# Long-context attention and a phase-mixing block: batch 0's q and k and the token weights turned by quarters of the array, and the opening put in another order

## The chip, the cores and the metric

The kernel runs on one core of one Trainium2 chip. Five engines work side by side, each through its own instructions in their written order: TensorE (PE, matmuls and transposes, with its weight loads shown apart as PEld), VectorE (DVE), ScalarE (ACT), GpSimd (POOL) and SyncE (SP). DMAs are issued from the queues of SP, ACT and POOL. The metric is device time in microseconds, lower is better. Three runs of the kernel before took 171.09, 171.58 and 172.12 us, so the median is 171.58.

## The reference

Inputs are q, k, v of shape [4 batches, 8 heads, 768 positions, 64], the weights w_theta and w_ch [512, 512] and the token weights w_tok_r and w_tok_i [768, 768]. The output is float32 [4, 768, 512].

```
scores = q @ k^T / 8 - slope[h] * dist        # keep: the first 8 keys, and the 96 keys up to the query
a      = softmax(where(keep, scores, -1e9));  x = a @ v, heads side by side: [4, 768, 512]
theta  = x @ w_theta;  zr = x*cos(theta);  zi = x*sin(theta)
y      = w_tok_r @ zr + w_tok_i @ zi          # over positions
u      = x + y;  out = u + relu(u @ w_ch)
```

## The kernel before

Positions are tiled by 128 (NT = 6 tiles), heads by pairs, so a pair of heads fills 128 partitions. Each batch goes through attention, theta, the token mix and the channel mix. Batches 1 to 3 run their attention beside the token mix of the batch before (`attend_beside`); batch 0's attention, its theta stage and the setup of the token weights stand alone at the beginning, in an order written out by hand (lines 533 to 603). All calls go through `K = tc.keep_in_program_order`, so each engine executes in the order of the source.

For each pair of heads, `att_transpose` (line 209) turns q and k with PE transposes into PSUM tiles `ps_tr` (two buffers) and copies them to the SBUF tile `qk`, reordering positions. For batch 0 (lines 238 to 250) one PSUM tile holds q and one holds k; each is filled by 12 transposes of 128x64, ACT copies k and DVE copies q. For later batches (lines 216 to 237) the array is used in quarters: 48 transposes of 64x64, one PSUM tile for each half of the partitions, each tile holding half of q and half of k. `att_extras` (line 254) then copies the middle key tiles with the 8 global keys put in front (`mT`), on POOL as a rule.

`att_scores` (line 279) works in three groups of score blocks. Group 0 needs `kT` and `qT` alone, groups 1 and 2 need `mT` as well. In batch 0, groups 0 and 2 get the distance bias by a matmul (`att_bias`, line 266, with `ident_d` as weights) and ACT's exp gives the probabilities; group 1 gets exp on ACT and then a product with `wmask` on DVE (`att_mul`, line 311). Scores lie in the wide PSUM tiles `ps_w` (two buffers). `prepare_v` (line 88) copies v for the same global keys. `att_values` (line 325) multiplies probabilities and v into `ps_mm` (two buffers), `att_norm` (line 358) divides on DVE, `turn_x` (line 368) transposes x for `mix_theta` (line 387). `mix_z` (line 407) forms z on DVE from ACT's sines.

`setup_wtok` (line 108) turns one 128-row strip `st` of a token matrix by six 128x128 transposes and copies it by one copy, on DVE for the first matrix and parts of the second, on ACT for strips 0 and 1 of the second. `mix_tok` (line 421) consumes the strips. In the order written out, the transposes of one lot lie between matmuls that need an earlier lot.

Loads go mostly by POOL's queue, which also computes; the first pair's q and k come by SP's and ACT's queues (line 141). `keep_warm` issues matmuls on zeros.

Of the kernel before, what the change touches and what calls it, by code (L numbers as in the profile page):

```python
# [10 lines left out]
BF = mybir.dt.bfloat16  # L11
# [5 lines left out]
def kernel(  # L17
# [13 lines left out]
    nc = tc.nc  # L31
    B, H, S, D = q.shape
    T = 128
# [74 lines left out]
    def setup_wtok(wi, st, eng, spare):  # L108
        if not spare:
            pt = ps_tr(S)  # L110
        else:
            pt = psum.tile([T, S], BF, name="ps_mm", tag="ps_mm", bufs=2)
        for tt in range(NT):
            K(nc.tensor.transpose(pt[:, tt * T:(tt + 1) * T],  # L114
                                  w_nats[wi][:, tt, st * T:(st + 1) * T], ident))
        if eng == "dve":
            K(nc.vector.tensor_copy(out=w_tokT[wi][:, st, :], in_=pt))  # L117
        else:
            K(nc.scalar.copy(out=w_tokT[wi][:, st, :], in_=pt))
# [21 lines left out]
    for src, dst, queue in ((q, first[:, 0], nc.sync), (k, first[:, 1], nc.scalar)):  # L141
        K(queue.dma_start(out=dst, in_=src[0, 0:2].rearrange("h (p t) d -> p h (t d)", t=NT)))
# [7 lines left out]
    keep_warm(8)  # L150
# [58 lines left out]
    def att_transpose(b, h0, extras=True, sins=None, q_eng="dve", between=None, cuts=(T,)):  # L209

        qk = abuf.tile([T, 2 * S + (NT - 2) * T], BF, name="qk", bufs=2)
        kT, qT = qk[:, 0:S], qk[:, S:2 * S]
        qTs[b, h0], kTs[b, h0] = qT, kT
        mTs[b, h0] = qk[:, 2 * S:]
        copy = nc.scalar.copy if q_eng == "act" else nc.vector.tensor_copy
        if b > 0:

            HP = T // 2
            halves = [ps_tr(S), ps_tr(S)]
            for t_ in range(NT):  # L220
                for i_, src in enumerate((k_sb[b], q_sb[b])):
                    c = (i_ * NT + t_) * HP
                    for r in range(2):
                        P = slice(r * HP, (r + 1) * HP)
                        for hh in range(2):
                            K(nc.tensor.transpose(  # L226
                                halves[r][hh * D:(hh + 1) * D, c:c + HP],
                                src[P, h0 + hh, t_ * D:(t_ + 1) * D], ident[P, P]))
            if sins is not None:
                sins()  # L230
            for r, op in enumerate((nc.scalar.copy, copy)):
                K(op(out=qk[:, 0:2 * S].rearrange("a (i r p t) -> a i r p t",  # L232
                                                  i=2, r=2, t=NT)[:, :, r, :, :],
                     in_=halves[r].rearrange("a (i t p) -> a i p t", i=2, t=NT)))
            if extras:
                att_extras(b, h0)
            return
        pq, pk = ps_tr(S), ps_tr(S)
        for src, pst in ((q_sb[b], pq), (k_sb[b], pk)):
            if pst is pk and between is not None:  # L240
                between()
            for t_ in range(NT):
                for hh in range(2):
                    K(nc.tensor.transpose(pst[hh * D:(hh + 1) * D, t_ * T:(t_ + 1) * T],
                                          src[:, h0 + hh, t_ * D:(t_ + 1) * D], ident))

        for op, dst, src in ((nc.scalar.copy, kT, pk), (copy, qT, pq)):
            for p0, p1 in zip((0,) + cuts, cuts):
                K(op(out=dst.rearrange("a (p t) -> a p t", t=NT)[:, p0:p1, :],  # L249
                     in_=src.rearrange("a (t p) -> a p t", t=NT)[:, p0:p1, :]))  # L250
        if extras:
            att_extras(b, h0)

    def att_extras(b, h0, eng=nc.gpsimd, values=True):
        kT = kTs[b, h0]
        mT = mTs[b, h0]
        K(eng.tensor_copy(out=mT, in_=kT[:, T:S - T]))  # L257
        K(eng.tensor_copy(
            out=mT.rearrange("a (t p) -> a t p", p=T)[:, :, 0:NG],
            in_=kT[:, None, 0:NG].to_broadcast([T, NT - 2, NG])))  # L260
        if eng is nc.gpsimd and values:
            prepare_v(b, h0)
# [16 lines left out]
    def att_scores(b, h0, g_, mul=True):  # L279
# [3 lines left out]
        bias = b == 0 and g_ != 1  # L283
# [249 lines left out]
    for h in range(H):  # L533
        make_wmask(h)
# [3 lines left out]
    att_transpose(0, 0, extras=False, between=lambda: keep_warm(1), cuts=(43, T))  # L538
    make_ident_d(2, 6)
    att_extras(0, 0, nc.vector)  # L540
    prepare_v(0, 0, nc.vector)
    keep_warm(1)
    att_scores(0, 0, 0)
    att_scores(0, 0, 1)
    att_transpose(0, 2, extras=False)
# [4 lines left out]
    for h0 in (2, 4, 6):  # L550
        att_scores(0, h0, 0)
        att_scores(0, h0, 1, mul=False)
        att_values(0, h0 - 2, apart=True)
        att_norm(0, h0 - 2)
        att_norm(0, h0 - 1)
        if h0 < 6:
            att_transpose(0, h0 + 2)
            if h0 == 2:
                load_wtok(1)
            else:  # L560
                load_heads(1, 0, 4)
        att_mul(0, h0, 1)
        att_scores(0, h0, 2)
        if h0 < 6:
            turn_x(0, h0 // 2 - 1, False)
# [101 lines left out]
```

## Time and profile before

| what | value |
|---|---|
| median of three runs | 171.58 us (171.09 to 172.12) |
| the profiled execution's own time | 171.33 us |
| its span, first to last instruction | 169.5 us |
| granted TensorE clock | 1.0 |
| busy: PE, DVE, ACT, POOL | 158.7, 114.7, 103.0, 63.2 us |
| DMA moved | 24.08 MB, mean 142 GB/s |
| first scores of batch 1 begin | 39.47 us |

The profile is of one execution. A line of the timeline gives start, duration, engine, source line, operation, output tile and input tiles, how many instructions were merged, and in brackets the idle time before the first of them with what ended it. The chain of waits follows the end of the program back to its start: each piece is work, or the idle time that the next piece had to wait for ("issue"). A time to landing is counted from a DMA's issue. Busy shares are averages over stages with different limits.

### The profile page before, as it was taken

To read this page: it belongs to the slowest core of one execution; us is meant where nothing else is said; L and a number is where in the kernel's file an instruction comes from. 1 tells how busy PE (TensorE), PEld (TensorE's weight loads), DVE (VectorE), ACT (ScalarE), POOL (GpSimd) and SP (SyncE) were. 2 spreads that over 40 slices of the span, in tenths; PEclk is the share of its full clock that TensorE was granted. 3 is DMA by queue.
4 is the path that set the end of the run, shared out by engine and by line. 5 is a ranking of instruction groups with operands and counts; after the bars stand their busy time and mean duration, and the time that the engine had idled before them with its cause. 6 is when DMAs were issued, how large, how long until landed. Compare 5 with 4: busy or idle time off the path is not lost.

```text
span 169.5 us, 4624 instructions
## 1 busy us (share of the span) xinstructions
PE 158.7 (94%) x1965; PEld 86.2 (51%) x1988; DVE 114.7 (68%) x210; ACT 103.0 (61%) x120; POOL 63.2 (37%) x99
## 2 busy tenths in 40 slices
PE   7779999999899999999999999999999999999992
PEld 2346665555465654446555554445655544444440
DVE  7768875965858875767587694849568756534362
ACT  4989887957686562798658615996765618300010
POOL 8996797004484650032972900054245000000000
PEclk9999999999999999999999999999999999999999
DMA  4999999999999999910599999711953342121325
GB/s 148 194 180 190 209 211 208 198 180 182 158 140 196 141 173 215 257 70 4 92 145 170 155 187 197 210 62 37 73 110 95 99 148 86 68 60 34 113 102 186
DMA packets 57060, 24.08 MB, mean 142 GB/s; under 512 B 43088, under 2 KB 54096, under 8 KB 57040
## 3 DMA queue, kind: packets, MB, share of 16 engines
q0 software_dynamic: 35328, 12.45, 65.5%
q1 hardware_dynamic: 21440, 10.95, 31.2%
q10 hardware_dynamic: 272, 0.39, 0.7%
q8 instruction: 15, 0.25, 0.6%
q14 instruction: 5, 0.04, 0.1%
HBM read 25.69 MB, written 6.29 MB: 189 GB/s over the span
## 4 chain that ended last, share of the span: by engine, by line
PE 80%; DVE 6%; DMA 4%; issue 3%; POOL 3%; ACT 3%; DVEq 0%; ACTq 0%; POOLq 0%
PE ps_mm L430 35%; PE ps_mm L472 12%; PE ps_w L395 11%; PE ps_w L297 7%; PE ps_w L346 5%; DMA v_sb<-in_v_dram 4%; PE ps_tr L226 3%; PE ps_mm L346 2%; ACT e L306 2%; PE ps_tr L114 2%; DVE zri L411 1%; DVE w_tokT L117 1%; PE ps_tr L378 1%; DVE p L319 1%; ACT qk L249 1%
## 5 line engine op out<-in xcount | busy, mean ns | idle before, releaser
L430 PE MATMUL ps_mm<-zri,w_tokT 128*128 128x512 bf16 x276 | 67.0, 380 | 1.3 <-issue 0.8
L306 ACT ACTIVATE e<-ps_w 128x1024 bf16<-128x1024 f32 (+1 forms) x40 | 37.1, 958 | 17.8 <-PE ps_w L297 17.8
L430 PEld LDWEIGHTS <-w_tokT 128*128 128x128 bf16 x288 | 26.2, 98 | 30.3 <-issue 2.3
L257 POOL COPY qk<-qk 128x512 bf16<-128x512 bf16 x15 | 9.5, 636 | 65.2 <-ACT qk L232 53.0
L319 DVE TENSOR_TENSOR p<-e,wmask 128x1024 bf16<-128x1024 bf16 x28 | 19.9, 712 | 11.8 <-ACT e L306 11.8
L403 ACT ACTIVATE cs<-ps_w,halfpi 128x1024 bf16<-128x1024 f32 x12 | 13.4, 1116 | 18.6 <-PE ps_w L395 18.6
L435 DVE TENSOR_TENSOR u<-x_sb,ps_mm 128x512 bf16<-128x512 bf16 x24 | 16.2, 683 | 12.2 <-PE ps_mm L430 12.2
L395 PE MATMUL ps_w<-w_theta_bf,xT 128*128 128x512 bf16 x91 | 22.6, 379 | 0.6 <-ACT cs L404 0.3
L411 DVE TENSOR_TENSOR zri<-cs,x_sb 128x1024 bf16<-128x1024 bf16 x24 | 16.1, 688 | 9.1 <-ACT cs L403 7.7
L472 PE MATMUL ps_mm<-w_ch_bf,uTd 128*128 128x512 bf16 x82 | 21.5, 379 | 0.6 <-issue 0.5
L297 PE MATMUL ps_w<-qk 64*128 64x128 bf16 (+1 forms) x320 | 16.1, 223 | 2.3 <-DVE qk L249 0.8
L475 DVE SCALAR_TENSOR_TENSOR o_sb<-ps_mm,u 128x512 f32<-128x512 f32 (+2 forms) x25 | 16.5, 664 | 1.1 <-PE ps_mm L472 0.9
L232 ACT COPY qk<-ps_tr 128x768 bf16<-128x768 bf16 x21 | 16.0, 815 | 2.0 <-issue 2.0
L297 PEld LDWEIGHTS <-qk 64*128 64x128 bf16 x320 | 10.0, 94 | 12.1 <-issue 7.8
L346 PEld LDWEIGHTS <-p 128*128 128x128 bf16 x352 | 13.2, 97 | 4.6 <-DVE p L319 0.8
L395 PEld LDWEIGHTS <-xT 128*128 128x128 bf16 x96 | 9.0, 98 | 10.8 <-issue 0.5
L80 POOL DMA_DIRECT2D v_sb<-in_v_dram x10 | 13.0, 1299 | 0.0
L472 PEld LDWEIGHTS <-uTd 128*128 128x128 bf16 x88 | 8.2, 98 | 9.0 <-issue 0.2
L404 ACT ACTIVATE cs<-ps_w 128x1024 bf16<-128x1024 f32 x12 | 12.2, 1020 | 0.0
L92 POOL COPY v_pv<-v_sb 8x520 bf16<-8x520 bf16 x15 | 11.5, 767 | 0.9
L354 DVE TENSOR_TENSOR x_sb<-ps_w,rec 128x768 bf16<-128x768 f32 x12 | 11.5, 958 | 0.4
L346 PE MATMUL ps_w<-v_sb,p 128*128 128x65 bf16 x168 | 11.3, 193 | 0.0
(84 smaller groups left out, 180.2 us busy)
## 6 DMA issues: line engine op xcount, KB each, us to landing
out_dram<-o_sb SPq DMA_DIRECT2D x23, 256.0 KB, 2.3
q_sb<-in_q_dram POOLq DMA_DIRECT2D x6, 384.0 KB, 6.2
k_sb<-in_k_dram POOLq DMA_DIRECT2D x6, 384.0 KB, 9.0
v_sb<-in_v_dram POOLq DMA_DIRECT2D x6, 384.0 KB, 13.5
w_nat<-in_moe_w_tok_r_dram POOLq DMA_DIRECT2D x1, 1152.0 KB, 12.3
w_nat<-in_moe_w_tok_i_dram POOLq DMA_DIRECT2D x1, 1152.0 KB, 13.4
v_sb<-in_v_dram POOLq DMA_DIRECT2D x4, 192.0 KB, 6.7
q_sb<-in_q_dram POOLq DMA_DIRECT2D x3, 192.0 KB, 5.9
```

Source lines behind the costliest of these rows:

```text
L232: K(op(out=qk[:, 0:2 * S].rearrange("a (i r p t) -> a i r p t", i=2, r=2, t=NT)[:, :, r, :, :], in_=halves[r].rearrange("a (i t p) -> a i ...
L297: K(nc.tensor.matmul(ps[:, hh, i_ * T:(i_ + w) * T], lhsT=keys[R, :], rhs=qT[R, it * T:(it + w) * T], start=not bias, stop=not bias or i_ ...
L306: K(nc.scalar.activation(e[:, :, 0:n * T], ps[:, :, 0:n * T], AF.Exp, scale=scale))
L319: K(nc.vector.tensor_mul(p.rearrange("a h (r x) -> a h r x", r=2), e.rearrange("a h (r x) -> a h r x", r=2), wmask[:, hs, None, T:3 * T].t ...
L346: K(nc.tensor.matmul(dst, lhsT=lhsT, rhs=rhs, start=(i_ == 0), stop=(i_ == len(mms) - 1)))
L395: K(nc.tensor.matmul(pth[:, s2, :], lhsT=xTs[b][:, dc, c:c + T], rhs=w_theta_bf[:, dc, :], start=(dc == 0), stop=(dc == NC - 1)))
L403: K(nc.scalar.activation(cs[:, :, 0, :], pth, AF.Sin, bias=halfpi))
L411: K(nc.vector.tensor_mul(zris[b][:, st:st + 2, wi, :].rearrange("a s (c d) -> a s c d", d=T), cs[:, :, wi, :].rearrange("a s (c d) -> a s ...
L430: K(nc.tensor.matmul(acc, lhsT=w_tokT[wi][:, st, tt * T:(tt + 1) * T], rhs=zris[b][:, st, wi, :], start=(done[b, tt] == 0), stop=(done[b, ...
L435: K(nc.vector.tensor_add(us[b][:, tt, :].rearrange("a (c d) -> a c d", d=T), x_sb[b][:, :, tt, :], acc.rearrange("a (c d) -> a c d", d=T)))
L472: K(nc.tensor.matmul(pc[:, 0:N], lhsT=uT[:, c:c + T], rhs=w_ch_bf[:, dc, cols], start=(dc == 0), stop=(dc == NC - 1)))
L475: K(nc.vector.scalar_tensor_tensor(o_sb, in0=pc[:, 0:N], scalar=0.0, in1=us[b][:, tt, cols], op0=ALU.max, op1=ALU.add))
```

## The change

The first pair's q and k are loaded in halves, one head each, q's two halves first, on the SP and the ACT queue. In batch 0 q and k are now turned in quarters, as in the later batches: q's 24 quarters first, then k's 24. The copies that came in two cuts for the first pair are whole. Six masks instead of eight are made ahead of the first scores, the others later; `ident_d` is made in three lots. A pair's transposes stand directly behind the second scores of the pair before, ahead of its values; `prepare_v` of pair 0 stands behind the first product on DVE. The last pair's group 0 uses `wmask` instead of the bias. Two of the turns of x stand later, and the third is copied by DVE. The token weights are turned two strips at a time in quarters: 48 transposes of 64x64 into two tiles, each holding half of the positions of both strips, and two copies. The order of the setup is written anew.

```
-        if not spare:
-            pt = ps_tr(S)
-        else:
-            pt = psum.tile([T, S], BF, name="ps_mm", tag="ps_mm", bufs=2)
...
+    def setup_wtok(wi, st0, engs, spare=False):
+        HP = T // 2
+        halves = [psum.tile([T, S], BF, name="ps_mm", tag="ps_mm", bufs=2) if spare else ps_tr(S)
+                  for _ in range(2)]
+        for s_ in range(2):
+            for tt in range(NT):
+                o = (s_ * NT + tt) * HP
+                for r in range(2):
+                    P = slice(r * HP, (r + 1) * HP)
+                    for c in range(2):
+                        col = (st0 + s_) * T + c * HP
+                        K(nc.tensor.transpose(halves[r][c * HP:(c + 1) * HP, o:o + HP],
+                                              w_nats[wi][P, tt, col:col + HP], ident[P, P]))
+        for r, eng in enumerate(engs):
+            op = nc.scalar.copy if eng == "act" else nc.vector.tensor_copy
+            dst = w_tokT[wi][:, st0:st0 + 2, :].rearrange("a s (t r p) -> a s t r p", r=2, p=HP)
+            K(op(out=dst[:, :, :, r, :],
+                 in_=halves[r].rearrange("a (s t p) -> a s t p", s=2, t=NT)))
...
-    for src, dst, queue in ((q, first[:, 0], nc.sync), (k, first[:, 1], nc.scalar)):
-        K(queue.dma_start(out=dst, in_=src[0, 0:2].rearrange("h (p t) d -> p h (t d)", t=NT)))
+    for src, dst in ((q, first[:, 0]), (k, first[:, 1])):
+        for hh, queue in enumerate((nc.sync, nc.scalar)):
+            K(queue.dma_start(out=dst[:, hh, :],
+                              in_=src[0, hh].rearrange("(p t) d -> p (t d)", t=NT)))
...
-    keep_warm(8)
+    keep_warm(7)
...
+        halves = [ps_tr(S), ps_tr(S)]
+        for i_, src in ((1, q_sb[b]), (0, k_sb[b])):
+            if i_ == 0 and between is not None:
                 between()
             for t_ in range(NT):
+                c = (i_ * NT + t_) * HP
+                for r in range(2):
+                    P = slice(r * HP, (r + 1) * HP)
+                    for hh in range(2):
+                        K(nc.tensor.transpose(
+                            halves[r][hh * D:(hh + 1) * D, c:c + HP],
+                            src[P, h0 + hh, t_ * D:(t_ + 1) * D], ident[P, P]))
...
+    def att_extras(b, h0, eng=nc.gpsimd, values=True, parts=1):
+        kT, mT = kTs[b, h0], mTs[b, h0]
+        n = (NT - 2) // parts
+        for t0 in range(0, NT - 2, n):
+            dst = mT[:, t0 * T:(t0 + n) * T]
+            K(eng.tensor_copy(out=dst, in_=kT[:, (t0 + 1) * T:(t0 + 1 + n) * T]))
+            K(eng.tensor_copy(
+                out=dst.rearrange("a (t p) -> a t p", p=T)[:, :, 0:NG],
+                in_=kT[:, None, 0:NG].to_broadcast([T, n, NG])))
...
-        bias = b == 0 and g_ != 1
+        bias = b == 0 and (g_ == 2 or g_ == 0 and h0 < H - 2)
...
-    for h in range(H):
+    for h in range(6):
         make_wmask(h)
...
     att_bias(0, 0)
-    att_transpose(0, 0, extras=False, between=lambda: keep_warm(1), cuts=(43, T))
-    make_ident_d(2, 6)
-    att_extras(0, 0, nc.vector)
+    att_transpose(0, 0, extras=False, between=lambda: keep_warm(1))
+    keep_warm(1)
+    att_extras(0, 0, nc.vector, parts=2)
+    make_ident_d(2, 2)
+    att_scores(0, 0, 0)
+    make_wmask(6)
+    att_scores(0, 0, 1, mul=False)
+    att_transpose(0, 2, extras=False)
+    att_mul(0, 0, 1)
     prepare_v(0, 0, nc.vector)
-    keep_warm(1)
-    att_scores(0, 0, 0)
-    att_scores(0, 0, 1)
-    att_transpose(0, 2, extras=False)
+    make_ident_d(4, 4)
     att_extras(0, 2, nc.gpsimd, False)
     prepare_v(0, 2)
     load_wtok(0)
     att_scores(0, 0, 2)
-    for h0 in (2, 4, 6):
+    for h0 in (2, 4):
         att_scores(0, h0, 0)
         att_scores(0, h0, 1, mul=False)
+        att_transpose(0, h0 + 2)
+        if h0 == 2:
+            make_wmask(7)
+            load_wtok(1)
+        else:
+            load_heads(1, 0, 4)
         att_values(0, h0 - 2, apart=True)
+        att_mul(0, h0, 1)
         att_norm(0, h0 - 2)
         att_norm(0, h0 - 1)
...
         att_scores(0, h0, 2)
+        if h0 == 4:
+            turn_x(0, 0, False)
+    att_scores(0, 6, 0)
+    att_scores(0, 6, 1, mul=False)
+    turn_x(0, 1, False)
+    att_values(0, 4, apart=True)
+    att_norm(0, 4)
+    att_norm(0, 5)
+    att_mul(0, 6, 1)
+    att_scores(0, 6, 2)
...
-    turn_x(0, 2, False, nc.scalar.copy)
+    turn_x(0, 2, False)
...
+    setup_wtok(0, 0, ("dve", "dve"))
     mix_z(0, 0)
+    setup_wtok(0, 2, ("dve", "dve"), True)
+    mix_theta(0, 4)
     mix_z(0, 2)
+    setup_wtok(0, 4, ("dve", "dve"))
     mix_tok(0, 0, [(st, 0) for st in range(4)])
     mix_tok(0, 1, [(st, 0) for st in range(4)])
+    setup_wtok(1, 0, ("act", "act"))
     mix_z(0, 4)
     mix_tok(0, 0, [(0, 1), (1, 1)])
     mix_tok(0, 1, [(0, 1), (1, 1)])
+    setup_wtok(1, 2, ("act", "dve"))
+    mix_tok(0, 0, [(4, 0), (5, 0)])
+    mix_tok(0, 1, [(4, 0), (5, 0)])
     att_transpose(1, 0)
+    mix_tok(0, 0, [(2, 1), (3, 1)])
+    mix_tok(0, 1, [(2, 1), (3, 1)])
+    setup_wtok(1, 4, ("dve", "dve"))
```

## The prediction, made before the result was known

> **What bounds the kernel now.** The page's busy shares come first, then the chain of waits in order of time, then each engine's timeline up to 45 us, then the times to landing of the loads.
>
> ```profile
> PE 158.7 (94%) x1965; PEld 86.2 (51%) x1988; DVE 114.7 (68%) x210; ACT 103.0 (61%) x120; POOL 63.2 (37%) x99
> ```
>
> TensorE (PE) works 94% of the span, and from 44 us on the chain is almost PE alone: what delays the first scores of batch 1 (line 297, 39.47 us) comes out at the end one for one. The change touches only what lies before. The chain there:
>
> ```profile
> 11.18 0.88 DVE qk L249
> 12.10 0.56 PE ps_w L297 x12
> ...
> 14.32 0.81 ACT qk L249
> 15.13 0.05 issue
> 15.19 0.62 POOL qk L257
> 15.86 0.56 POOL qk L258
> 16.47 0.40 PE ps_w L297 x8
> ...
> 28.20 0.37 DVE w_tokT L117
> ...
> 32.56 0.48 DVE w_tokT L117
> 33.04 0.04 issue
> 33.08 0.96 PE ps_tr L114 x12
> 34.04 0.86 PE ps_mm L430 x4
> 34.90 0.76 PE ps_tr L114 x12
> 35.66 0.05 issue
> 35.71 0.81 PE ps_mm L430 x3
> 36.52 0.51 PE ps_tr L226 x48
> 37.03 0.16 issue
> ```
>
> Two stages are seen. In batch 0's attention each pair of heads goes turn, copy, POOL copy, group-1 scores, so the next group-1 scores wait for POOL; one round lasts 16.47 to 20.75 = 4.28. From 28.20 to 33.04 DVE sets the pace, and then PE turns the second token matrix in small lots between matmuls with almost no gap. From the timeline:
>
> ```profile
> 33.61 1.50 ACT L119 COPY w_tokT<-ps_tr 128x768 bf16<-128x768 bf16 x2
> 37.12 0.80 ACT L232 COPY qk<-ps_tr 128x768 bf16<-128x768 bf16 x1 [2.01 <-issue]
> 37.94 1.28 ACT L306 ACT_TABLE_LOAD   x1
> 28.68 0.55 DVE L117 COPY w_tokT<-ps_mm 128x768 bf16<-128x768 bf16 x1
> 18.74 0.95 DVE L249 COPY qk<-ps_tr 128x768 bf16<-128x768 bf16 x1
> 39.23 1.02 DVE L117 COPY w_tokT<-ps_tr 128x768 bf16<-128x768 bf16 x2 [1.09 <-PE ps_tr L114]
> ```
>
> The first line is the cover to watch: while ACT copies, PE has four matmuls and twelve turns to do.
>
> **The change, part by part.** *First loads.* q landed at 0.74 + 4.5 = 5.24, k at 0.74 + 4.8 = 5.54. Halves on two queues bring q before k; bounds are no gain, or q at half the transfer (about 4.6) with k as before. ACT issues a second DMA of about 0.49, so its table load ends near 3.2 instead of 2.75, hidden because line 193 waits for DVE until 3.61. One keep_warm less brings the bias to 4.3 (ident_d is ready at 4.27). q turns are then done before k's cast, which starts at 5.6 rather than 5.73. All of k's turns still precede both copies, and without the cut the first scores wait for a 0.80 copy instead of 0.375: about 7.6 against 7.79. Group 1 waits for half the DVE extras, then ACT does one mask (0.43) before its exp, at 9.1 against 9.25. This gain of 0.15 ends there: POOL issues loads until 10.9 and only then copies pair 2's keys (11.03 to 11.93), in both kernels. Its queue keeps its order, SP's too.
>
> *The stall on v.* DVE now copies pair 2 before prepare_v, so v's landing (9.33) no longer holds it: group 0 of pair 2 runs at 10.9, ahead of POOL, and group 1 at 11.98 instead of 12.44. prepare_v (1.2) and four ident_d (0.6) end on DVE at 12.5, before values 0 at 13.0 need them.
>
> *Quarters for q and k.* 24 turns of line 244 take 0.79 (17.57 to 18.36); 48 of line 226 take 0.51 and 0.16 idle, 0.67: 0.12 saved per pair. The copies keep their prices (0.80 ACT, 0.95 DVE).
>
> *Turns behind the second scores.* Laying the rows end to end from 11.98: group 1 0.39, turns 0.66, values 0.78, group 2 0.86, next group 0 0.77 gives 15.45; POOL's copies for pair 4 end at 15.4, so that wait (0.20) is gone. Group 1 of pair 4 is at 15.5 against 16.47, of pair 6 at 19.3 against 20.75 (here ACT copies pair 6 behind two exps until 18.05 and POOL ends at 19.25: PE idles 0.46). Lead 1.4. Pair 4's k landed at 5.96 + 6.2 = 12.2 and pair 6's at 8.38 + 7.0 = 15.4; they are needed at 12.6 and 16.1, so loads just hold.
>
> *What eats the lead.* DVE now sets the pace: from 16.55 copy 0.87, product 0.63, norms 1.40, turn 0.47, the new product for pair 6 (0.56; it saves PE 0.43 of bias), turn 0.47, norms 1.40, product 0.65, with small waits, ends at 23.15. values 6 wait for that product, then thetas, and turn 3 is at 25.25 against 25.95. Lead 0.7. The third turn's copy on DVE (0.55 for 0.80 on ACT) fits behind values 6.
>
> *Token weights.* 48 quarters 0.67, 12 whole turns 0.67: PE gains nothing. But a pair's two copies each need all 48, where a copy used to start after six (0.34). The DVE chain (copies, z, copies, z) starts at 27.9, not 28.2: lead 0.3. The trace shows no DVE copy that writes runs of 64 and reads in one piece. Bounds: 0.55 of line 117 and 0.95 of line 249. The nearest row is 117, since 249 differs in reading with a stride; I take 0.55 and keep 0.95 as a rival. [...]
>
> *The new order.* The DVE copies of weights 0/4 end 5.3 after the chain's start, 33.2, and free the buffers for the first pair of the second matrix: turned 33.2 to 33.87, copied twice on ACT (0.75 spacing, 1.50 in all, latencies 0.1) to 35.5. Next in PE's program are matmuls on just this pair. The eight matmuls that used to lie beside are already spent: PE idles 1.6. Queued behind: four matmuls 0.86, turns 0.67, four matmuls 0.86 (37.9), batch 1's q and k turns 0.67, four matmuls 0.86, wait for their DVE copy (39.6), last turns 0.67: 40.3 against 39.47. Batch 1's exp shifts the same, its table load (1.28) starting at the end of the copy, 39.4. Then the last pair's two DVE copies, 40.3 to 41.3, precede the matmuls on weights 4 and 5: 41.35, where the second matmul had waited until 40.25. Group-1 scores of batch 1 follow at 41.75 against 40.64.
>
> Sum: -0.7 in the opening; +0.4 because copies await 48 quarters; +0.45 at the second matrix's start, which needed one DVE copy out of the way and now needs both; +0.7 from there to batch 1's first scores (33.2 to 40.3 is 7.1, 33.08 to 39.47 was 6.4: the idle 1.6 less gaps that go); +0.25 for the last copies: +1.1. The profiled execution took 171.33 (span 169.5 and 1.8 around it), so 172.4; it lay 0.25 below the median 171.58, which gives 172.7. I say 172.5.
>
> [...]
>
> **The rivals.** A, the forecast: +1.1, its own bounds +0.5 to +1.8 (how far the 1.6 is covered, how much lead arrives). B, the opening's lead arrives nearly whole: DVE's work alone from 13.05 sums to 11.5, so turn 3 could be at 24.6, 0.65 earlier than reckoned; for it speaks that products cost 0.60 when POOL is still, against it the waits between. +0.45, 171.8. C, not slower: PE doesn't idle at 33.9, because the four matmuls on weights 4 and 5 of the first matrix and the next turns get ahead of the waiting ones. Their inputs are ready by 34.4. It decides from the point where 1.1 of the 1.6 is filled; filled wholly, -0.5, 170.8. Against it: rows 33.08 to 36.52 run exactly as written. D, the 64-runs copy at 0.95: six copies of DVE's chain and the last two take 0.4 more each, 8 x 0.4 = 3.2 on top, 175.6. E, pair 4's or 6's loads are late (slack 0.4 and 0.7): an added 0.5, 172.9; their landings ride on a queue busy throughout, against it that nothing is issued earlier on POOL.
>
> **How the numbers follow.** A 0.52, B 0.17, C 0.11, D 0.10, E 0.10. A change within 0.5% (0.86 us) is about what a measurement can't tell from none. Slower: A above +0.86 (0.38), D, E most: 0.56. Same: the rest of A (0.14), B nearly all, part of C: 0.34. Faster: the low end of C and of B: 0.10. The range 170.7 to 174.0 leaves out D (0.10) and that low end of C (0.05); A alone spans 171.8 (+0.5 on the profiled execution) to 173.4 (+1.8 on the median).
>
> **What would show it.** Right: group-1 scores of pair 2 near 12.0, of pair 6 near 19.3; turn 3 near 25.3; weight copies on DVE at 0.55; PE idle about 1.6 at 33.9 with ACT's weight copy as releaser; batch 1's first scores near 40.3. Wrong: no such idle (C), weight copies near 0.95 (D), a DMA releasing line 244's successor (E), or an opening that ends over 1.3 earlier, which would mean DVE did not take over.

## The result, and the profile after

The changed kernel took 176.01 us (median of six runs, 174.9 to 177.39) against 171.83 for the kernel before (six runs, 171.09 to 172.19): 1.0254 times as long, interval 1.0208 to 1.03. The direction was forecast; the size, +1.1, was a quarter of the true one, and 176.0 lies outside the range. The ratios, here and below, leave out executions that ran far slower than the rest of their kernel, so a ratio can lie below what its median says.

The page after, its busy times and, from the list of DMA queues, the instruction queue q8 (packets, MB, share; a second such queue, q14, has 5 packets in both kernels):

```profile
PE 162.7 (93%) x2297; PEld 84.5 (48%) x2297; DVE 115.2 (66%) x212; ACT 102.5 (59%) x119; POOL 63.1 (36%) x99
...
q8 instruction: 18, 0.29, 0.7%
```

The same queue of the kernel before:

```profile
q8 instruction: 15, 0.25, 0.6%
```

PE's share is as high as it was, so the page's first part tells nothing of the loss. The small lines tell more: PE has 4594 recorded rows (matmuls and weight loads) where it had 3953, because a turn in quarters takes four times the instructions, and q8 fetched three more packets of 16 KB.

The chain of waits after, in order of time (start, us, what):

```profile
12.16 0.45 PE ps_w L294 x4
12.63 0.81 ACT p L299
...
16.57 0.40 PE ps_w L294 x8
...
34.29 0.45 PE ps_tr L120 x24
34.73 1.49 ACT w_tokT L125 x2
...
36.27 1.04 PE ps_mm L427 x4
...
38.01 1.82 PE ps_mm L427 x4
39.83 0.79 PE ps_tr L235 x27
40.62 1.07 PE ps_mm L427 x4
41.70 0.71 PE ps_tr L120 x48
42.41 1.01 DVE w_tokT L125 x2
```

Two links are as written in the forecast: ACT's copies of the second matrix's first pair (34.73) and DVE's last pair (42.41) now stand in the chain. In between, four matmuls of 128x512 take 1.82 where four such took 0.86 before. The timeline shows the same stretch; DVE first, then PE, with idle time and its end in brackets:

```profile
28.57 1.02 DVE L125 COPY w_tokT<-ps_tr 128x768 bf16<-128x768 bf16 x2 [1.32 <-PE ps_tr L120]
```
```profile
9.04 0.54 PE L235 MATMUL ps_tr<-ident,q_sb 64*64 64x64 bf16 x24
...
16.90 0.38 PE L235 MATMUL ps_tr<-ident,q_sb 64*64 64x64 bf16 x24
...
36.27 1.04 PE L427 MATMUL ps_mm<-zri,w_tokT 128*128 128x512 bf16 x4 [1.60 <-ACT w_tokT L125]
...
37.95 1.89 PE L427 MATMUL ps_mm<-zri,w_tokT 128*128 128x512 bf16 x4
39.77 0.53 PE L235 MATMUL ps_tr<-ident,q_sb 64*64 64x64 bf16 x24
...
42.28 0.34 PE L294 MATMUL ps_w<-qk 64*128 64x256 bf16 x4
43.47 0.61 PE L427 MATMUL ps_mm<-zri,w_tokT 128*128 128x512 bf16 x2 [0.85 <-DVE w_tokT L125]
44.00 0.62 PE L294 MATMUL ps_w<-qk 64*128 64x128 bf16 x16
```

The forecast idle of 1.60 is there, and so is one of 0.85 behind DVE's last two copies. But there is also something that no term of the sum held: the same 24 quarters take 0.54 at 9.04, 0.53 at 39.77, and 0.38 at 16.90. By the trace's clock records the granted clock was first full (1.0) from 13.50 on (before: from 6.21), and half (0.5) from 37.39 to 40.80; ahead of the first full grant they have no entry, but the matmul rows change their pace at just these times. (The expectations below give the clock's times some 0.24 later.)

Where the 4.70 of the span went: the last of batch 0's four turns of x, the forecast's turn 3 (it counts from 0), came at 26.08 instead of 25.90 (+0.18); from there to batch 1's first scores it took 16.20 instead of 13.56 (+2.64); from the first to the second scores of batch 1 1.72 instead of 1.18 (+0.54); +0.93 came later, 0.76 of it PE's wait for a DMA transpose of u at 106.56; +0.41 came after the last matmul.

The last piece is no accident of one run: 3.74 to 3.79 lie behind the last matmul in every kernel with the new opening, 3.38 and 3.39 in the kernel before and in e7, which keeps the old one. At the end SP goes through nine waits for landings in a fixed order. Before, the last two outputs report to semaphores 117 and 118, which stand in the last two of these waits; after, they report to 100 and 102, which stand in the second and third, and the six waits behind take some 0.4 more. That the opening's two additional loads moved the numbers on by two is likely, but was not tried.

### The profile page after: what moved, and what is told of

It reads as the page before. It is cut to its first block, busy times and chain, and to the rows that moved or that the text cites. A ratio compares the mean times of both kernels' runs of the same rounds, so it can differ in the third digit from the quotient of the medians.

```text
span 174.2 us, 5277 instructions
## 1 busy us (share of the span) xinstructions
PE 162.7 (93%) x2297; PEld 84.5 (48%) x2297; DVE 115.2 (66%) x212; ACT 102.5 (59%) x119; POOL 63.1 (36%) x99
## 4 chain that ended last, share of the span: by engine, by line
PE 78%; DMA 8%; ACT 5%; DVE 4%; issue 2%; DVEq 0%; SPq 0%; ACTq 0%
PE ps_mm L427 35%; PE ps_w L392 11%; PE ps_mm L469 11%; PE ps_w L294 7%; DMA uTd<-u 5%; PE ps_w L343 5%; PE ps_tr L235 5%; DMA first<-in_k_dram 3%; PE ps_tr L120 2%; ACT e L303 1%; PE ps_w L273 1%; PE ps_tr L375 1%; DVE p L316 1%; DVE qk L243 1%; ACT p L299 1%
## 5 line engine op out<-in xcount | busy, mean ns | idle before, releaser
L427 PE MATMUL ps_mm<-zri,w_tokT 128*128 128x512 bf16 x288 | 69.5, 384 | 2.4 <-ACT w_tokT L125 1.6
L303 ACT ACTIVATE e<-ps_w 128x1024 bf16<-128x1024 f32 (+1 forms) x41 | 37.8, 954 | 17.3 <-PE ps_w L294 17.3
L254 POOL COPY qk<-qk 128x512 bf16<-128x512 bf16 x15 | 10.0, 669 | 69.3 <-ACT qk L243 55.1
L316 DVE TENSOR_TENSOR p<-e,wmask 128x1024 bf16<-128x1024 bf16 x28 | 19.3, 691 | 12.1 <-ACT e L303 12.1
L469 PE MATMUL ps_mm<-w_ch_bf,uTd 128*128 128x512 bf16 x88 | 22.5, 379 | 0.8 <-DMA uTd<-u 0.8
L243 ACT COPY qk<-ps_tr 128x768 bf16<-128x768 bf16 x25 | 19.2, 815 | 2.7 <-PE ps_tr L235 2.7
L294 PE MATMUL ps_w<-qk 64*128 64x128 bf16 (+1 forms) x320 | 17.1, 232 | 1.8 <-ACT p L299 0.9
L294 PEld LDWEIGHTS <-qk 64*128 64x128 bf16 x320 | 10.6, 97 | 12.7 <-issue 6.8
```

The source lines that it names most:

```text
L294: K(nc.tensor.matmul(ps[:, hh, i_ * T:(i_ + w) * T], lhsT=keys[R, :], rhs=qT[R, it * T:(it + w) * T], start=not bias, stop=not bias or i_ ...
L303: K(nc.scalar.activation(e[:, :, 0:n * T], ps[:, :, 0:n * T], AF.Exp, scale=scale))
L316: K(nc.vector.tensor_mul(p.rearrange("a h (r x) -> a h r x", r=2), e.rearrange("a h (r x) -> a h r x", r=2), wmask[:, hs, None, T:3 * T].t ...
L427: K(nc.tensor.matmul(acc, lhsT=w_tokT[wi][:, st, tt * T:(tt + 1) * T], rhs=zris[b][:, st, wi, :], start=(done[b, tt] == 0), stop=(done[b, ...
L469: K(nc.tensor.matmul(pc[:, 0:N], lhsT=uT[:, c:c + T], rhs=w_ch_bf[:, dc, cols], start=(dc == 0), stop=(dc == NC - 1)))
```

## The experiments

"Setup" is the time from turn 3 of x (the expectations call it the third turn) to batch 1's first scores, from each kernel's profiled execution; it was 13.56 in the kernel before. A whole time is a median, a ratio is to the kernel before on the same chip.

**Which part of the change costs.**

e1, the setup of before with the new opening:

```
-    setup_wtok(0, 0, ("dve", "dve"))
+    setup_one(0, 0, "dve", False)
+    setup_one(0, 1, "dve", True)
     mix_z(0, 0)
-    setup_wtok(0, 2, ("dve", "dve"), True)
+    setup_one(0, 2, "dve", False)
+    setup_one(0, 3, "dve", True)
...
```

> The changed kernel with the setup of the token weights as before (whole turns, strip by strip, the old order of turns and matmuls); the new opening stays. Theory: the loss sits in the new setup (PE idle 1.6 behind the ACT copies, then TensorE at half clock for 3.4 us, then the late last copies), and the opening, which got the full clock only at 13.7 us, gains nothing. Then batch 1's first scores come at about 39.7 us (before 39.47, changed 42.28) and the time is about 172.5. Rival: the loss is the opening's or that of loads and DMA transposes which now land at another time; then 174.5 or more remains.

173.4, ratio 1.0096 [1.0061, 1.0131]. Its setup took 13.56 again, so the new setup alone stands for most of the loss, 2.6 of 4.2. The rest is more than was expected (172.5): its turn 3 came only at 27.22.

e5, quartered token turns in the setup order of before, and e6, whole token turns in the new order:

```
     setup_wtok(0, 0, ("dve", "dve"))
     mix_z(0, 0)
     setup_wtok(0, 2, ("dve", "dve"), True)
-    mix_theta(0, 4)
     mix_z(0, 2)
+    mix_theta(0, 4)
...
     mix_tok(0, 0, [(st, 0) for st in range(4)])
+    setup_wtok(1, 0, ("act", "act"))
     mix_tok(0, 1, [(st, 0) for st in range(4)])
-    setup_wtok(1, 0, ("act", "act"))
     mix_z(0, 4)
...
```
```
         for s_ in range(2):
             for tt in range(NT):
-                o = (s_ * NT + tt) * HP
...
+                col = (st0 + s_) * T
+                K(nc.tensor.transpose(pts[s_][:, tt * T:(tt + 1) * T],
+                                      w_nats[wi][:, tt, col:col + T], ident))
+        for s_, eng in enumerate(engs):
...
+            K(op(out=w_tokT[wi][:, st0 + s_, :], in_=pts[s_]))
```

> New opening; token weights in quarters, two strips at a time, but turned and used in the order of the kernel before, so that matmuls lie beside the ACT copies again. Three kernels stopped PE for 0.9 to 1.9 us with no wait at the same matmul (about the 730th) until a 16 KB block on queue 8, begun near 38 us, had landed. New theory (PE runs out of instructions there, since quarters take 96 instructions for 24): no idle behind the ACT copies, but PE stops again near 39 us, batch 1's first scores at 41.5 or later, time about 175.5. Rival (the new order of the setup alone made the loss): no stop, first scores near 40, time about 173.7, as with the old setup (173.4).

> New opening and the new order of the setup, but the token weights turned whole (24 instructions for two strips instead of 96). New theory: the idle of about 1.6 behind the ACT copies stays, no stop for instructions; about 1.2 above the kernel with the old setup (173.4), so 174.6. Rival (quarters are the whole loss of the setup and the order costs nothing): 173.4. Rival (the order is the whole loss): 176.

e5: 176.68, ratio 1.0299 [1.0244, 1.0353], setup 16.12. e6: 174.1, ratio 1.0151 [1.0096, 1.0205], setup 14.41. The order costs 0.85 of setup with whole turns and next to nothing on top of quarters; the quarters cost 2.56 in the old order. In e6 the idle behind ACT splits, as each matmul waits for its own strip's copy alone:

```profile
35.13 0.39 PE L420 MATMUL ps_mm<-zri,w_tokT 128*128 128x512 bf16 x1 [0.56 <-ACT w_tokT L119]
35.83 0.82 PE L420 MATMUL ps_mm<-zri,w_tokT 128*128 128x512 bf16 x3 [0.31 <-ACT w_tokT L119]
```

e7, the kernel before with only batch 0's q and k in quarters, and e8, the new order of the opening with whole turns of q and k and the old setup:

```
-        pq, pk = ps_tr(S), ps_tr(S)
+        halves = [ps_tr(S), ps_tr(S)]
...
-                    K(nc.tensor.transpose(pst[hh * D:(hh + 1) * D, t_ * T:(t_ + 1) * T],
-                                          src[:, h0 + hh, t_ * D:(t_ + 1) * D], ident))
+                        K(nc.tensor.transpose(
+                            halves[r][hh * D:(hh + 1) * D, c:c + HP],
+                            src[P, h0 + hh, t_ * D:(t_ + 1) * D], ident[P, P]))
```

That is e7's edit; e8 is e1 with these lines taken back.

> The kernel before with one part of the change alone: batch 0's q and k in quarters (both copies whole), order of the opening, loads, masks and setup as before. If quarters are harmless there: 4 x 0.12 less PE and a first copy that ends later, so 171.4 against 171.7. If the full clock comes late or falls because quarters keep PE less busy, or instructions run short: 172.5 or more.

> The new opening (halved first loads, transposes behind second scores, last pair by the mask, fewer masks ahead) with batch 0's q and k turned whole, and the old setup. If the order gives the lead of 0.7 that was reckoned and quarters lost it: about 171.0, below the kernel before. If the order itself costs (PE idle before pair 2's group 1, then half clock): near 173.4, as with quarters.

e7: 174.1, ratio 1.0143 [1.0111, 1.0176], turn 3 at 28.42 (before 25.90). e8: 171.85, ratio 1.0023 [0.9994, 1.0053], turn 3 at 25.38. So quarters for q and k lose: some 2.5 in the old order (e7), 1.55 in the new one (e1 less e8). That the new order of the opening wins half a microsecond by itself is not shown: e12 below has the opening of e8, and its turn 3 came at 26.09, at full clock too. The reason for the loss in e7 is on POOL's timeline: one PSUM tile no longer holds k alone, so POOL's copy of the keys waits for both copies, DVE's too, for 1.70, 1.88 and 1.40 with pairs 2, 4 and 6 (before, for ACT alone, 1.24 and 1.04 with pairs 4 and 6):

```profile
12.59 0.61 POOL L243 COPY qk<-qk 128x512 bf16<-128x512 bf16 x1 [1.70 <-DVE qk L234]
```

In e1 PE waits for POOL as well ahead of pair 2's group 1, but for another reason: POOL was held up by a load, and DVE's copy had long ended, at 10.39.

```profile
12.64 0.40 PE L308 MATMUL ps_w<-qk 64*128 64x128 bf16 x8 [1.51 <-POOL qk L269]
```
```profile
10.80 0.75 POOL L102 DMA_DIRECT2D w_theta_bf<-in_moe_w_theta_dram  x1 [0.56 <-DMA v_sb<-in_v_dram]
11.55 0.77 POOL L268 COPY qk<-qk 128x512 bf16<-128x512 bf16 x1
```

e8 and e12, with whole turns, have this wait too (0.64 and 1.29). So the mechanism of e7 is shown for the old order; what costs the 1.55 in the new one is open.

**Is it the idle behind ACT, or the clock?** e2 puts four matmuls that are ready into the idle; e3 fills it with zero matmuls; e4 gives PE one more zero matmul at three places of the opening.

```
     mix_z(0, 4)
+    mix_tok(0, 0, [(4, 0), (5, 0)])
+    mix_tok(0, 1, [(4, 0), (5, 0)])
     mix_tok(0, 0, [(0, 1), (1, 1)])
-    mix_tok(0, 1, [(0, 1), (1, 1)])
     setup_wtok(1, 2, ("act", "dve"))
-    mix_tok(0, 0, [(4, 0), (5, 0)])
-    mix_tok(0, 1, [(4, 0), (5, 0)])
+    mix_tok(0, 1, [(0, 1), (1, 1)])
```
```
     mix_z(0, 4)
+    keep_warm(7, ps_wide()[:, 0, :])
     mix_tok(0, 0, [(0, 1), (1, 1)])
```
```
-    keep_warm(7)
+    keep_warm(8)
...
-    att_transpose(0, 0, extras=False, between=lambda: keep_warm(1))
-    keep_warm(1)
+    att_transpose(0, 0, extras=False, between=lambda: keep_warm(2))
+    keep_warm(2)
```

> The changed kernel, with the four matmuls on strips 4 and 5 of the first matrix put ahead of the matmuls on the second matrix's first pair, and that pair's matmuls split around the next turns. Theory (the idle behind the ACT copies, and the clock drop that follows it, make the loss of the setup): idle 0.7 instead of 1.6, no half clock near 38 us, first scores of batch 1 at about 40.5, time about 174.2. Rival (quarters are slow in themselves, or the loss is elsewhere): first scores stay near 42, time near 176.

> The changed kernel with seven matmuls on zeros put into the idle 1.6 us behind the ACT copies; nothing is taken from the path. Theory (the clock drop at 37.6 us comes from that idle time and costs some 1.2 us of its own): no half clock between 34 and 42 us, first scores at about 41.1, time about 174.8. Rival (the clock falls because quarter turns do not keep it up, whatever stands in the gap): half clock still there, no change, 176.

> The changed kernel with three more matmuls on zeros in the opening (8, 2 and 2 instead of 7, 1 and 1), in PE time that was idle or waited for ident_d and k. Theory (the full clock came at 13.7 instead of 6.4 us because the opening keeps PE less busy, and this ate the lead of 0.7): full clock before 10.5 us, third turn of x near 25.3 instead of 26.1, time about 175.2. Rival (DVE bounds the opening, the clock does not matter there): full clock early, third turn still at 26.1, time 176.

e2: 177.03, ratio 1.0196 [1.0144, 1.0247]; the idle fell to 0.63, PE stood still for 1.87 at 38.99, and the first scores came at 42.77. e3: 177.69, ratio 1.0366 [1.0323, 1.0408], the clock full from 6.53 to the last microseconds, and still first scores at 42.03. e4: 176.96, ratio 1.0306 [1.0258, 1.0353], the half clock only moved, to 13.54 to 16.96. None gains; the theory that the idle and the clock dip make the loss fell with e3. The kernel after itself agrees: its profiled run has a mean granted clock of 0.989, which is the one stretch of 3.41 in a span of 174.2, but another of its six runs has 1.000, so no such stretch, and took 175.5 all the same. The PE timeline of e3 shows what stood behind them:

```profile
33.97 1.69 PE L144 MATMUL ps_w<-zero 128*128 128x512 bf16 x6
35.64 1.04 PE L427 MATMUL ps_mm<-zri,w_tokT 128*128 128x512 bf16 x4
...
38.29 0.32 PE L235 MATMUL ps_tr<-ident,k_sb 64*64 64x64 bf16 x17
40.13 0.25 PE L235 MATMUL ps_tr<-ident,k_sb 64*64 64x64 bf16 x7 [1.52 <-issue]
```

No semaphore, no other engine: PE stops in the middle of 24 turns whose inputs and outputs are all there.

**Is it the supply of instructions?** In every kernel with quartered token turns PE gets past about its 730th recorded matmul some 1.5 us (1.18 to 1.69 in the table) after a packet of the instruction queue has landed, whatever it is doing there (us, from the traces' DMA and matmul records; numbers of matmuls are good to some six, as a few records are missing; six of ten such kernels):

| kernel | packet begins, lands | PE stops for | goes on at |
|---|---|---|---|
| after | 38.20, 39.15 | none seen, matmuls at half clock | 40.33 |
| e3 | 37.63, 38.58 | 1.52 | 40.13 |
| e5 | 38.16, 39.11 | 1.31 | 40.64 |
| e9, loads late | 35.92, 37.08 | 0 | 38.63 |
| e16, fewer loads | 36.77, 37.82 | 0.47 | 39.40 |
| e18, fewer loads | 36.00, 37.12 | 0 | 38.81 |

While the DMA engines were full (busy share 0.9 or more from 4.4 to 43.6 us in the kernel after) the packets began some 6.3 us apart (after: 12.92, 18.84, 24.94, 31.92, 38.20, 44.42; e3: 12.40, 18.59, 24.52, 31.30, 37.63, 44.07). A packet is some 255 of PE's rows (an estimate: 4594 over 18), and 48 quarters use 96 of them in 0.6. The stops lie as far apart: counted in rows, every stop of PE over 0.25 that ends with nothing visible, in any of the kernels, comes near row 703, 1465 or 1720 and ends 1.3 to 1.6 after a packet has landed. e3 stops a second time at the last of these, for 1.45 until 46.32; the next packet had landed at 45.01. e9 and e18 reach the spot 1.55 and 1.69 after the landing as well, but without a stop: the packet came earlier. e9 takes away from e5 what may make the packets wait: the loads of batch 1's heads 4 to 7 and of w_ch are issued later. e11 does the same to e1, which has no quartered token turns.

```
-    load_heads(1, 4, 4)
-    load_weight(w_ch_bf, moe_w_ch)
     mix_theta(0, 0, 0, 2)
...
     att_transpose(1, 0)
+    load_heads(1, 4, 4)
+    load_weight(w_ch_bf, moe_w_ch)
```

> The kernel with the new opening, quartered token turns and the setup in the order of before (median 176.68, first scores of batch 1 at about 42.1), with one edit: the loads of batch 1's heads 4 to 7 and of w_ch (1.69 MB as bf16 on the chip) are issued behind the turns of batch 1's first pair, some 15 us later. Theory (TensorE stops at its matmul 730 and again near 856 because the next 16 KB of its instructions are fetched by the same DMA engines, which the loads keep full): the engines are empty from about 32 us, the blocks come as soon as they are wanted, both stops (1.32 and 1.01 us) go, and with the stall on the last copies smaller too the first scores of batch 1 come near 40.0. The time falls by about 2 us to some 174.5 unless the late loads hold up something behind them. Rival (the stops are the price of 64x64 transposes themselves, or of clock windows): the stops stay at the same matmuls and the first scores at 42 within 0.4.

> Control for the run with late loads: the same edit in the kernel with the new opening and the token setup of before (median 173.4), which has no stop of that kind. Theory: first scores of batch 1 move by less than 0.4 from the 40.8 of that kernel; the time shows what late loads alone do to the batches behind, between 172.5 and 174.5. Rival (late loads help whatever the turns are): the first scores come 1 us or more earlier here too.

e9's setup fell from 16.12 to 14.64, its first scores came at 40.09, and both stops are gone (e5's second, 1.01 until 47.38 and at the same row, the trace puts down to ACT's copy). e11's setup stayed at 13.57. First e5, then e9, PE's timeline at the same matmuls:

```profile
38.51 0.81 PE L427 MATMUL ps_mm<-zri,w_tokT 128*128 128x512 bf16 x3 [0.16 <-issue]
40.64 1.04 PE L427 MATMUL ps_mm<-zri,w_tokT 128*128 128x512 bf16 x4 [1.31 <-issue]
```
```profile
37.98 1.67 PE L427 MATMUL ps_mm<-zri,w_tokT 128*128 128x512 bf16 x7 [0.16 <-issue]
```

And the DMA engines from 36 to 46 us (40 slices, busy share in tenths), the kernel after and then e9:

```profile
DMA  9999999999999999999999999999999999997654
```
```profile
DMA  9974000000000000200000000099417999999999
```

The whole times, 185.72 and 185.77, are worthless for this question: w_ch came so late that PE waited 9.6 for it in e9. The expectation of 174.5 missed that. e13, e14 and e15 therefore leave w_ch where it was and move the heads alone, in e5, e1 and the kernel after:

```
-    load_heads(1, 4, 4)
     load_weight(w_ch_bf, moe_w_ch)
...
     att_transpose(1, 0)
+    load_heads(1, 4, 4)
```

> The kernel with the new opening, quartered token turns and the setup in the order of before (176.68), with only the loads of batch 1's heads 4 to 7 issued behind batch 1's first turns; w_ch stays where it was. Theory (instruction supply): no stop at TensorE's matmuls 730 and 856, first scores of batch 1 near 40.1 (42.1 without the edit), a wait of some 0.8 for the late k; time 174.5 to 175.5. Rival (what is won there is taken by waits behind): first scores at 40.1 and time within 0.6 of 176.7.

> Control: the same edit in the kernel with the new opening and the token setup of before (173.4, first scores 40.8). It has no stop to lose; what changes here is the price of loads that come late. Theory: first scores within 0.4 of 40.8, time 173.4 to 174.4 (0 to 1.0 for the late k). Rival (late loads shorten this kernel too): below 172.8.

> The same edit in the changed kernel itself (176.0, first scores 42.28 with 1.60 idle behind ACT's copies, 0.85 behind the last copies and a half clock from 37.6 to 41.0). Theory: the stop at matmul 730 goes (1.2 by its first scores' sister kernels), the idle behind ACT stays: first scores near 41, time 174.2 to 175.2. Rival (the idle behind ACT's copies and the supply lie beside each other, so one alone does not help): first scores at 42.0 or later and time within 0.5 of 176.0.

e13: 176.27, ratio 1.0281 [1.0255, 1.0307], setup 15.44, the first stop 0.76 and the second gone. e14: 176.86, ratio 1.0241 [1.0208, 1.0273], setup 13.56, but in its profiled run, 179.1, with waits of 1.81 for the late v and 1.09 for POOL's copy of it. e15: 176.7, ratio 1.0286 [1.0238, 1.0333], setup 15.75, stop 1.20. With w_ch alone the DMA engines stayed busy until after the packet had begun (38.45), so the stop shrank without going away, and late heads cost what was won. Nothing could be read from the end times, so the last three leave loads out (batch 1's pairs 4 and 6 then compute from other heads, and the output differs):

```
-    load_heads(1, 4, 4)
+    def src_head(b, h):
+        return h % 4 if b == 1 else h      # batch 1's pairs 4 and 6 read heads 0 to 3
...
     att_transpose(1, 0)
+    load_weight(w_ch_bf, moe_w_ch)
```

> New opening, quartered token turns, setup in the order of before (176.68 with all loads), but batch 1's heads 4 to 7 are not loaded: its pairs 4 and 6 compute from heads 0 to 3 instead, so the output differs and every engine's instructions are the same; w_ch is loaded behind batch 1's first turns. Theory (supply): no stop at matmuls 730 and 856, from the third turn of x to batch 1's first scores 14.6 (16.1 with all loads), and the time falls to 173.8 to 174.8, 1.0 to 1.5 above the sister kernel with whole token turns (3.3 above it with all loads). Rival: the setup takes 14.6 but the difference at the end stays 2.5 or more.

> New opening and the token setup of before (173.4 with all loads), with the same loads left out (pairs 4 and 6 of batch 1 compute from heads 0 to 3, so the output differs). Theory: from the third turn of x to batch 1's first scores 13.56 as ever; the time 172.2 to 173.4, whatever fewer loads save the transposes of u. Rival (loads slow every kernel alike): the setup becomes shorter by 0.5 or more here too.

> The changed kernel (176.0) with the same loads left out (the output differs in the same way). Theory: the stop at matmul 730 goes, but the idle of 1.6 behind ACT's copies and the wait of 0.9 behind the last copies stay: from the third turn of x to batch 1's first scores 15.0 to 15.4 (16.2 with all loads), time 174.2 to 175.2, above the run in the order of before by some 0.4. Rival (ACT's copies and the supply lie beside each other): setup of 16 and time near 175.6.

| kernel | all loads: time, setup | fewer loads: time, setup | difference in time |
|---|---|---|---|
| quarters, old order (e5, e16) | 176.68, 16.12 | 173.33, 15.15 | -3.35 |
| whole turns, old order (e1, e17) | 173.4, 13.56 | 172.44, 13.57 | -0.96 |
| the kernel after (after, e18) | 176.01, 16.20 | 176.58, 14.84 | see below |

The ratios: e16 1.0127 [1.0074, 1.018], e17 1.004 [1.0011, 1.0069], e18 1.0296 [1.0221, 1.0372]. Quartered token turns cost 3.28 at the end with all loads (e5 less e1) and 0.89 without them (e16 less e17); reckoned by the ratios it is 3.5 and 1.5. So 2.0 to 2.4 of it hangs on the loads that lie beside the turns; the kernel with whole turns gains only 1.0 when they are gone, and that part is none of the turns' doing. e18's profiled execution took 173.39 and shows the stop gone. Its other three runs took 175.5, 177.66 and 178.65; they have no trace; their mean granted clocks are 0.976, 0.978 and 0.970 against 0.997, so they lost time at half clock, but where is not known, and with a spread of 3% neither median nor ratio says much. So for the changed kernel itself the gain is shown in the setup (16.20 to 14.84) and not at the end; and as its profiled run had the half clock at this spot and e18's had not, that pair does not part the supply from the clock. e5 and e9, both at full clock there, do. e18's PE timeline is the forecast's own:

```profile
35.85 0.81 PE L431 MATMUL ps_mm<-zri,w_tokT 128*128 128x512 bf16 x3 [1.83 <-ACT w_tokT L129]
...
40.31 0.34 PE L298 MATMUL ps_w<-qk 64*128 64x256 bf16 x4
41.73 0.38 PE L431 MATMUL ps_mm<-zri,w_tokT 128*128 128x512 bf16 x1 [1.07 <-DVE w_tokT L129]
42.04 0.62 PE L298 MATMUL ps_w<-qk 64*128 64x128 bf16 x16
```

**What takes the rest.** e10 keeps PE busy in the opening of e1, and e12 issues the loads of batches 2 and 3 one piece of the token mix later in e8:

```
-    keep_warm(1)
+    keep_warm(4)
     att_extras(0, 0, nc.vector, parts=2)
...
         att_scores(0, h0, 0)
+        if h0 == 2:
+            keep_warm(7)
         att_scores(0, h0, 1, mul=False)
```
```
+                m(1)
                 if load and h0 == 0:
                     load_heads(b + 1, 0, 4)
                 if load and h0 + 4 == H:
                     load_heads(b + 1, 4, 4)
-                m(2)
+                m(1)
```

> The kernel with the new opening and the token setup of before (median 173.4, its runs lying in two groups near 172.4 and 174.2), with zero matmuls where TensorE idles: three more ahead of the first scores and seven ahead of pair 2's group 1 (idle 0.78 and 1.51). They occupy TensorE only where it waited, so they cost 0.2 at most. Theory (the half clock from 13.16 to 16.57 follows the idle stretches and costs the upper group its 1.7 us): no half clock between 7 and 40 us, third turn of x near 25.9 instead of 27.2, all runs near 172.4. Rival (the upper group is a late DMA transpose of u at 64 us): the time keeps both groups, median 173 to 174, whatever the clock shows.

> The kernel with the new order of the opening, whole turns of q and k and the token setup of before (median 171.85; its profile waited 0.39 and 1.62 for DMA transposes of u between 64 and 69 us), with batches 2 and 3's loads issued one piece of the token mix later. Theory (what the opening wins, 0.5 at batch 1's first scores, is lost where the transposes of u stand behind these loads): the wait of 1.62 falls below 0.6 and the time is 171.0 to 171.5, ahead of the kernel before. Rival (loads that come later only move the collision to the next transpose, or make the next batch's first pair late): 171.6 to 172.5, with a wait of over 1 us for a transpose of u or a load.

e10: 173.1, ratio 1.0051 [1.0022, 1.0079]. The half clock is gone as expected, but turn 3 came only at 26.76, and the runs keep two groups (five from 172.27 to 172.48, seven from 173.01 to 174.04): the rival was right. Its profiled run, 174.04, waits 1.28 for a transpose of u. e12: 172.51, ratio 1.001 [0.9985, 1.0034]: the rival again; its profiled run, 175.65, has three such waits, 3.2 in all. That of e8 took 173.78, 1.9 more than its median, and has this wait:

```profile
68.53 1.04 PE L497 MATMUL ps_mm<-w_ch_bf,uTd 128*128 128x512 bf16 x4 [1.62 <-DMA uTd<-u]
```

Why the usual run of e8 is no faster than the kernel before is thus not shown. The profiled kernel before has no such wait. Of the kernels with the new opening all but e18 show one, between 0.2 and 3.2, and e7 has 0.33; which transfer holds the transpose up was not settled. No version here beats the kernel before.

## Why the prediction was right or wrong

*First loads, group 0 and group 1.* Forecast 7.6 for the first scores, 9.1 for ACT's exp, and 11.98 for pair 2's group 1; the kernel after had 8.06, group 1's first matmul at 8.50, and 12.71. The order of events was right. The durations were taken from rows at full clock, and until 13.50 the rows ran at the pace of the half clock (24 quarters in 0.54 at 9.04, as in 0.53 at 39.77, not 0.38). Where the clock was full early, pair 2's group 1 came at 12.11 (e3, e18).

*Lead of 1.4 eaten by DVE down to 0.7.* The chain after indeed runs over DVE from 17.63 to 20.59. Turn 3 came at 26.08 instead of 25.25, and the lead was smaller all the way: group 1 of pair 4 at 16.57 instead of 15.5, of pair 6 at 20.19 instead of 19.3. Where the clock was full from 7.1 or earlier on, kernels with this opening had turn 3 between 25.47 and 25.72 (e3, e16, e17, e18): the reckoning was 0.2 to 0.5 short at full clock. Six with a half clock somewhere from 12.5 to 17.3 (e1, e4, e11, e13, e14, e15) had it between 26.46 and 27.48. So the lead went mostly where the clock was half; but e10, with a full clock and ten zero matmuls more, had it at 26.76, and e8 and e12, with one opening and a full clock, lie 0.7 apart, so the clock is not shown to be the cause.

*Quarters for q and k save 0.12 a pair.* This step failed. It priced PE's time, and left out that POOL's key copies now need DVE's copy as well as ACT's: 1.70 of wait in e7, where the quarters alone, and a half clock of 6.83 beside them, put turn 3 of x 2.52 later. In the new order they cost 1.55 of the whole time (e1 less e8), and what does it there is open.

*Token quarters: PE gains nothing, copies at 0.55, +0.4.* The copies were right (1.02 for two, not 0.95 each), so rival D is out. PE was not held up by the copies of the first matrix: its one idle time there, 0.73 ahead of 29.70, ended with ACT's sine. "48 quarters 0.67, 12 whole turns 0.67" is the step that failed: as a time on PE it held (0.58 to 0.82 for 48), but 48 turns are 96 instructions in place of 24, and near 38 us instructions came no faster than the packets (some 6.3 apart). That put the supply of instructions at nothing. The runs showed it at 1.48 of the setup in the old order (16.12 against 14.64 in e9, where whole turns did not move: 13.56 and 13.57). In the kernel after the same spot was run at half clock, and it passed there 1.2 to 1.4 after the packet's landing without a stop: two limits lay upon each other. At full clock the supply alone held e3 to a setup of 16.45; with neither limit e18 took 14.84 in place of 16.20.

*The new order: PE idles 1.6, first scores 40.3, group 1 at 41.75, +0.7 and +0.25.* The idle was 1.60, so rival C is out. The times were 42.28 and 44.00; in e18, which has all of the changed order but a freer supply, 40.31 and 42.04, with an idle of 1.83, and the other signs near the forecast: group 1 of pair 2 at 12.11, of pair 6 at 19.30, turn 3 at 25.48. The forecast's setup was 40.3 less 25.25, 15.05; e18's was 14.84. The mechanism was right; of the 2.64 by which the setup grew it is the 1.28 that e18 keeps.

*E, loads late.* In the kernel after PE waited for no load of batch 0's pairs 4 and 6; how thin the slack was shows in e3, which waits 0.21 for k of pair 6, and in e14, 0.21 and 0.61 for q and k of pair 4. Loads did harm by another way, the instruction queue.

*After 44 us one for one.* The chain was said to be PE alone from there, so a delay would come out as it is. The delay at batch 1's second scores was 3.36 and at the end 4.70; the 0.76 for a transpose of u and 0.41 after the last matmul were in no term.

Of the sum's own terms the new order and the copies were found again. The 3.6 of the span that it lacked lie in four places: 0.9 in the opening (+0.18 for a lead of 0.7; cause open), 1.1 in the setup (the supply, with the half clock upon it), 0.3 at the last copies, and 1.3 behind 44 us. The direction was no luck: with the supply freed, the setup of e18 is still 1.28 longer than before.

## What to carry to other kernels

Turning in smaller tiles cost instructions (96 for 24) where it cost no PE time (0.58 to 0.82 for 48 quarters, 0.83 for 12 whole turns in e6); count them, and look at whether the DMA engines are full just where they are to be fetched (1.48 here, e5 less e9). A tile that mixes two tensors made its reader wait for both copies (1.70 in e7). An idle stretch that has a visible releaser may hide a second limit behind it (in e3 the idle was filled, and PE stopped for 1.52 further on): fill the idle in an experiment before giving it the whole loss.

## What the runs showed of the hardware

The instruction queue q8 brought packets of 16 KB (18 in the kernel after, 15 before), one for some 255 rows of PE (an estimate: 4594 over 18; before 3953 over 15, 264). Under full DMA engines they began some 6.3 us apart in the kernel after and e3; in the kernel before, with fewer rows, at 16.00, 22.12, 30.67, 41.90 and 47.42. Where PE had stopped (e3, e5, e16) it went on 1.3 to 1.6 after one had landed: work did not hide 1.31 of the wait in e5 and 1.52 in e3, and hid all of it in e9, where the DMA engines ran empty at 37 us.

The half clock (0.5 by the clock records) came in stretches of 3.41 us (after, e1, e4, e5, e6), 6.83 (e2, e7), 10.24 (e9) or 13.65 (e11), and its place changed from kernel to kernel (37.39 to 40.80 in the kernel after, 13.54 to 16.96 in e4). Why the first full grant came at 13.50 in one kernel and at 6.53 in another with the same opening (e3) no run separates.
